# One decode step of attention and a gated feed-forward block: a 224-byte tile below the big slots, and eight tiny loads around the first rows of w_down

## The chip, the core and the metric

The kernel runs on one core of a Trainium2 chip. The metric is the device time of one execution in microseconds (us). Of the kernel before, three runs gave 1369.99, 1370.03 and 1370.04 us, so the median is 1370.03 us. One further execution was taken with the hardware profiler; every duration, wait and load below comes from that one, unless another kernel is named.

## The reference

One token `x` (1 x 576, float32) goes through a layer norm, and the result feeds two blocks whose outputs are added to `x`:

```python
xn = _layernorm(x)
q = (xn @ wq) in 32 heads of 128
p = softmax(q . k_cache * 128**-0.5)        # k_cache: 32 x 16384 x 128
o = (p . v_cache) @ wo                      # v_cache: 32 x 16384 x 128, wo: 4096 x 576
h = gelu(xn @ w_gate) * (xn @ w_up)         # 576 x 4608 each
return x + o + h @ w_down                   # w_down: 4608 x 576
```

Everything is float32. The two caches are 268 MB each, so nearly all of the 588 MB that the kernel reads is read once, used for one or two operations per element, and dropped.

## The kernel before, in words

**Memory.** Small tiles live in one pool (`cpool`) that is allocated first. Behind it lie three big slots of 64 KB in each of the 128 partitions: two from `kpool` (`kslot()`, line 62) and one from `vpool` (`vslot()`, line 65). With the small tiles of this version, the slots begin at byte 27,680 of each partition. 27,680 is 108 x 256 + 32; as every big load starts in its slot at a multiple of 256 bytes and has rows of a multiple of 256 bytes, all of them start 32 bytes past a multiple of 256.

**Loads.** Every big load is one DMA issued by SyncE (SP) through `load` (line 68), and all of these stand in one queue. A load of one head of K or V is 8192 KB: 128 rows, one for each partition, of 65,536 bytes. Sixteen DMA engines take eight rows each, and each engine ends its share by writing the load's semaphore, a packet of 4 bytes. 81 big loads are issued in all.

**Semaphores.** The compiler takes eight DMA semaphores in turn for the loads. A load whose semaphore was last used by a load that nobody is known to have waited for is held back on SP until that earlier load has landed. A load into a slot also waits until the slot's last reader is done.

**Heads.** The loop at line 249 goes over the 32 heads. VectorE multiplies the K slot by the query (`qk`, line 215) and sums it up over 128 elements (line 216), some 17.2 us each; the softmax follows (lines 218 to 230); TensorE then multiplies the V slot by the probabilities (`pv`, line 236), some 10 us. K of head h+1 and V of head h are under way meanwhile. The last head's V goes into a K slot, since no further K follows.

**The end.** Lines 291 to 297 load `w_down` and `wo` into the three slots as they come free. In order: 28 of the 36 row blocks of `w_down` into the V slot (`ta`, 8064 KB), its last 8 into a K slot (`tb`, 2304 KB), 16 row blocks of `wo` behind them (4608 KB), and 8, 4, 2, 1 and 1 row blocks of `wo` into the other K slot (`te`), which holds the last V until `pv` is done with it. Lines 299 to 310 normalise the attention's outputs and turn them into a column (`pot`, then `oT`), lines 312 to 325 multiply `w_down` and `wo` row block by row block on TensorE (`add_out`, line 281), and line 328 copies the sum out for the last DMA, which ScalarE issues.

Of the kernel before, what the change touches and what calls it, by code (L numbers as in the profile page):

```python
# [8 lines left out]
F32 = mybir.dt.float32  # L9
# [4 lines left out]
P = 128  # L14
# [20 lines left out]
QUART = D // 4  # L35
HG = 4
PW = 4 * HG
QH = 4


@with_exitstack
def kernel(ctx: ExitStack, tc: tile.TileContext, x, k_cache, v_cache, wq, wo, wg, wu, wd, out):
    nc = tc.nc
    cpool = ctx.enter_context(tc.tile_pool(name="cpool", bufs=1))
# [15 lines left out]
    wdv = wd.rearrange("(p t) f -> p (t f)", t=WD_T)  # L60

    def kslot():
        return kpool.tile([P, R * DH], F32, tag="k", name="kslot")

    def vslot():
        return vpool.tile([P, R * DH], F32, tag="v", name="vslot")

    def load(dst, src):
        nc.sync.dma_start(dst, src)  # L69
        return dst  # L70
# [5 lines left out]
    row3, tails, at = {}, {}, 0  # L76
# [73 lines left out]
    def q_spread(h):  # L150
        r = 32 * (h // (H // 4))
        lo = h % (H // 4) * DH
        pq = ps_s.tile([P, 512], F32, tag="sm", name="pq")
        nc.tensor.matmul(pq, ones[r : r + 1, :], qrow[r : r + 1, lo : lo + QH * DH], start=True, stop=True)  # L154
        return pq

    def q_take(h, pq):
        qs = spool.tile([P, QH, DH], F32, name="qs", bufs=1)
        nc.scalar.activation(qs.rearrange("p h d -> p (h d)"), pq, AF.Copy)
        for i in range(QH):  # L160
            Q[h + i] = qs[:, i : i + 1, :]
# [41 lines left out]
    S, KT, VT = {}, {}, {}  # L203
    pe = cpool.tile([P, PW - 4 + 32 * PW], F32, name="pe")
    nc.vector.memset(pe, 0.0)
    pe4 = pe[:, PW - 4 :].rearrange("p (k s) -> p k s", s=PW)[:, :, :4]
    lsum = cpool.tile([P, H], F32, name="lsum")
    oall = cpool.tile([P, H], F32, name="oall")

    def qk(h, i, n):  # L210
# [21 lines left out]
    def pv(h):  # L232
        vt, i = VT.pop(h), h % HG
        for k in range(32):
            q, lo = 32 * (k % 4), k * PW + PW - 4 - 4 * i
            nc.tensor.matmul(PO[h // HG % 2][q : q + PW, :], pe[:, lo : lo + PW], vt[:, k * 512 : (k + 1) * 512],  # L236
                             start=i == 0 and k < 4, stop=i == HG - 1 and k >= 28)

    def out_heads(h):
        o4 = spool.tile([P, 512], F32, name="o4", bufs=1)  # L240
        nc.scalar.activation(o4, PO[h // HG % 2], AF.Copy)  # L241
        pc = ps_s.tile([P, 512], F32, tag="sm", name="pc")
        pick = same[:, :PW].rearrange("p (i j) -> p j i", j=4)
        for j in range(4):
# [4 lines left out]
    for h in range(H + 1):  # L249
# [4 lines left out]
        if h > 0:  # L254
            VT[h - 1] = load(vslot() if h < H else kslot(), vv[h - 1])
        more = (h + 1) % QH == 0 and h + 1 < H
        pq = q_spread(h + 1) if more else None
# [29 lines left out]
    def load_rows(t, at, src, lo, n):  # L287
        load(t[:, at * D : (at + n) * D], src[:, lo * D : (lo + n) * D])
        return [t[:, (at + j) * D : (at + j + 1) * D] for j in range(n)]

    ta, tb, te = vslot(), kslot(), kslot()
    a, b = WD_PIECES
    wd_rows = load_rows(ta, 0, wdv, 0, a) + load_rows(tb, 0, wdv, a, b)
    wo_rows, lo = [], 0
    for n in WO_PIECES:
        wo_rows += load_rows(tb, b + lo, wov, lo, n) if lo < WO_A else load_rows(te, lo - WO_A, wov, lo, n)
# [61 lines left out]
```

## Time and profile before

| What | us |
|---|---|
| median of three runs | 1370.03 |
| the profiled execution's own time | 1370.16 |
| its span, first to last instruction | 1368.3 |
| VectorE busy within the span | 1135.8 (83%) |
| TensorE matmuls busy | 406.0 (30%) |
| ScalarE busy | 36.5 (3%) |

The span is 1.9 us shorter than the execution's own time. The page of the profile lists busy times, the DMA engines' share, the DMA queues, and the chain of work that ended last: followed back from the last instruction, at each step to what released it. The chain in order of time gives a start, a duration and what it was; the piece "DMA kslot<-in_A_k_cache_dram" is the time for which nothing but that transfer was being waited for. The timeline gives instructions with the idle time before them and what ended it. The DMA view can be narrowed to a stretch of time; its columns are a queue and its kind, the number of packets that began in the stretch, their MB, and the time that they took as a share of sixteen engines' time in that stretch (so one packet can take over 100% of a very short one).

### The profile page before, as it was taken

The numbers are of one execution on the slowest core, as the hardware profiler recorded it, in microseconds if no ns is written. First come the engines' busy times: TensorE is split into PE (matmuls) and PEld (weight loads), VectorE is DVE, ScalarE is ACT, GpSimd is POOL, SyncE is SP. The second block draws the span as 40 slices with busy tenths as digits, with TensorE's granted clock in tenths as the row PEclk, the third lists the DMA queues.
The fourth block names the chain that finished last, engine by engine and source line by source line (L and its number), as shares of the span: only waits on it lengthen the run. The fifth ranks groups of instructions, "written<-read, shape, count | busy, mean of one in ns | idle before, by whom it ended". The sixth has DMA issues, their size and how long they took to land.

```text
span 1368.3 us, 6377 instructions
## 1 busy us (share of the span) xinstructions
PE 406.0 (30%) x2870; PEld 118.1 (9%) x2870; DVE 1135.8 (83%) x169; ACT 36.5 (3%) x126; POOL 1.0 (0%) x7
## 2 busy tenths in 40 slices
PE   4321233322311232323212332322213333221156
PEld 1110000100000000100000000100001000000012
DVE  1069999899888888898888888998888888988840
ACT  0000000000000000000000000000000000000000
POOL 0000000000000000000000000000000000000000
PEclk8775565565556556565566566565556555665577
DMA  9999999999999999999999999999999999999997
GB/s 404 440 425 450 430 429 430 430 435 432 437 435 429 431 430 439 432 432 435 431 436 433 433 431 430 435 432 439 435 430 430 431 432 437 438 435 428 429 428 336
DMA packets 11704, 588.00 MB, mean 430 GB/s; under 512 B 1303, under 2 KB 1309, under 8 KB 1694
## 3 DMA queue, kind: packets, MB, share of 16 engines
q1 hardware_dynamic: 11664, 587.60, 99.4%
q8 instruction: 22, 0.36, 0.1%
q14 instruction: 4, 0.03, 0.0%
q10 hardware_dynamic: 14, 0.01, 0.0%
HBM read 587.60 MB, written 0.00 MB: 429 GB/s over the span
## 4 chain that ended last, share of the span: by engine, by line
DMA 51%; DVE 46%; PE 2%; issue 0%; SPq 0%; ACT 0%; DVEq 0%
DMA kslot<-in_A_k_cache_dram 41%; DVE s L216 23%; DVE kslot L215 23%; DMA kslot<-in_A_v_cache_dram 3%; DMA kslot<-in_B_w_up_dram 3%; DMA kslot<-in_A_wo_dram 3%; DMA kslot<-in_A_wq_dram 2%; PE pg L139 1%; PE po L236 1%; DVE gu L179 0%; SPq L69 0%; PE pt L222 0%; DVE vslot L176 0%; DVE pm L220 0%; DVE nm L224 0%
## 5 line engine op out<-in xcount | busy, mean ns | idle before, releaser
L215 DVE TENSOR_TENSOR kslot<-kslot,qs 128x16384 f32<-128x16384 f32 (+1 forms) x33 | 551.3, 16705 | 88.4 <-DMA kslot<-in_A_k_cache_dram 86.9
L216 DVE TENSOR_REDUCE s<-kslot 128x128 f32<-128x16384 f32 (+1 forms) x33 | 551.2, 16703 | 3.3
L236 PE MATMUL po<-vslot,pe 128*16 128x512 f32 x1984 | 286.1, 741 | 645.0 <-DMA vslot<-in_A_v_cache_dram 645.0
L236 PEld LDWEIGHTS po<-vslot,pe 128*16 128x16 f32 x1984 | 67.3, 113 | 848.2 <-issue 848.2
L222 PE MATMUL pt<-ident,pm 128*1 128x128 f32 x32 | 11.9, 372 | 236.0 <-DVE pm L220 236.0
L176 DVE TENSOR_TENSOR vslot<-pg,same 128x396 f32<-128x396 f32 (+1 forms) x6 | 3.0, 552 | 69.1 <-PE pg L139 69.1
L139 PE MATMUL pg<-kslot,xnb 128*32 128x396 f32 (+2 forms) x208 | 23.6, 615 | 33.6 <-DMA kslot<-in_B_w_gate_dram 18.9
L228 ACT ACTIVATE nb<-pb 128x1 f32<-128x1 f32 x32 | 5.5, 171 | 812.4 <-PE pb L226 812.4
L320 DVE TENSOR_TENSOR x<-x,po 64x288 f32<-64x288 f32 x1 | 0.5, 457 | 30.8 <-PE po L281 30.8
L222 PEld LDWEIGHTS pt<-ident,pm 128*1 128x1 f32 x32 | 2.5, 79 | 259.4 <-DVE pm L220 218.5
L226 PE MATMUL pb<-nm,ones 1*128 1x1 f32 x64 | 18.1, 350 | 13.2 <-DVE nm L224 13.2
L224 DVE TENSOR_REDUCE nm<-pt 1x1 f32<-1x128 f32 x32 | 8.9, 278 | 14.9 <-PE pt L222 14.9
L226 PEld LDWEIGHTS pb<-nm,ones 1*128 1x128 f32 x64 | 15.8, 305 | 22.2 <-DVE nm L224 11.3
L154 PE MATMUL pq<-qrow,ones 1*128 1x512 f32 x16 | 15.6, 1073 | 0.0
L229 ACT ACTIVATE pe<-s,nb 128x128 f32<-128x128 f32 x32 | 12.8, 401 | 1.0
L302 DVE RECIPROCAL rl<-pl 128x32 f32<-128x32 f32 x1 | 0.4, 358 | 14.9 <-PE pl L300 14.9
L281 PE MATMUL acc<-kslot,oT 128*1 128x144 f32 (+1 forms) x112 | 10.5, 376 | 6.7 <-DMA kslot<-in_A_wo_dram 6.7
L139 PEld LDWEIGHTS pg<-kslot,xnb 128*32 128x32 f32 x208 | 7.1, 126 | 51.0 <-DMA kslot<-in_B_w_gate_dram 19.7
L241 ACT ACTIVATE o<-po 128x512 f32<-128x512 f32 x8 | 4.8, 597 | 222.0 <-PE po L236 222.0
L236 PE MATMUL po<-kslot,pe 128*16 128x512 f32 x64 | 9.6, 769 | 2.6 <-DMA kslot<-in_A_v_cache_dram 2.6
L281 PE MATMUL acc<-vslot,hT 128*1 128x288 f32 x56 | 8.6, 473 | 5.6 <-DMA vslot<-in_B_w_down_dram 5.6
L245 PE MATMUL pc<-same,o 128*128 128x4 f32 x64 | 8.4, 255 | 5.7 <-ACT o L241 5.7
(74 smaller groups left out, 109.9 us busy)
## 6 DMA issues: line engine op xcount, KB each, us to landing
kslot<-in_A_k_cache_dram SPq DMA_DIRECT2D x2, 4096.0 KB
vslot<-in_B_w_down_dram SPq DMA_DIRECT2D x1, 8064.0 KB
kslot<-in_B_w_gate_dram SPq DMA_DIRECT2D x1, 6912.0 KB, 54.0
kslot<-in_B_w_up_dram SPq DMA_DIRECT2D x1, 6912.0 KB
kslot<-in_A_wo_dram SPq DMA_DIRECT2D x1, 4608.0 KB, 39.2
vslot<-in_B_w_gate_dram SPq DMA_DIRECT2D x1, 2304.0 KB, 28.9
vslot<-in_B_w_up_dram SPq DMA_DIRECT2D x1, 2304.0 KB, 37.6
kslot<-in_B_w_down_dram SPq DMA_DIRECT2D x1, 2304.0 KB, 28.7
```

The source lines that it names most:

```text
L139: nc.tensor.matmul(pg[32 * q : 32 * q + 32, b, :size], lhs, rhs[:, lo : lo + size], start=k == 0, stop=k == len(steps) - 1)
L154: nc.tensor.matmul(pq, ones[r : r + 1, :], qrow[r : r + 1, lo : lo + QH * DH], start=True, stop=True)
L215: tc.keep_in_program_order(nc.vector.tensor_mul(blk, blk, Q[h].to_broadcast([P, n, DH])))
L216: nc.vector.tensor_reduce(S[h][:, i : i + n], blk, axis=AX.X, op=ALU.add)
L222: nc.tensor.transpose(pt[:1, :P], pm, ident)
L224: tc.keep_in_program_order(nc.vector.tensor_reduce(nm, pt[:1, :P], axis=AX.X, op=ALU.max, negate=True))
L226: nc.tensor.matmul(pb[:, :1], ones[:1, :], nm, start=True, stop=True)
L228: nc.scalar.activation(nb, pb[:, :1], AF.Copy, scale=SCALE)
L229: nc.scalar.activation(pe4, S.pop(h).rearrange("p (k s) -> p k s", s=4), AF.Exp, bias=nb, scale=SCALE, accum_out=lsum[:, h : h + 1])
L236: nc.tensor.matmul(PO[h // HG % 2][q : q + PW, :], pe[:, lo : lo + PW], vt[:, k * 512 : (k + 1) * 512], start=i == 0 and k < 4, stop=i == ...
L245: nc.tensor.matmul(pc[:, :HG], o4[:, j * DH : (j + 1) * DH], pick[:, j, :], start=j == 0, stop=j == 3)
L281: nc.tensor.matmul(g, lhs, w[:, i * n : (i + 1) * n], start=id(g) not in seen, stop=last)
```

## The change

A tile `pad` of 128 x 56 floats (224 bytes in each partition) is taken from the small tiles' pool. The slots so move up by 224 bytes to byte 27,904, which is 109 x 256.

Eight loads into `pad` are added to the SP queue, which nothing reads. The load with number n takes the first n rows of `w_down` and writes them to partitions 0, 4, 8 and so on; n floats of each row (8 to 32 bytes), and 17 floats (68 bytes) for n = 1. Numbers 1 to 4 stand between the last V and the 28 row blocks of `w_down`, numbers 5 to 8 between these and the last 8. A scheduler orders the instructions of the other engines; the eight loads are held where the program has them. In the built program one matmul changes its place beside that: TensorE's first multiplication of a `w_down` row now stands ahead of the `pot` matmul of line 308 instead of behind it.

```diff
+PAD = 56
...
     lsum = cpool.tile([P, H], F32, name="lsum")
+    pad = cpool.tile([P, PAD], F32, name="pad")
     oall = cpool.tile([P, H], F32, name="oall")
...
     ta, tb, te = vslot(), kslot(), kslot()
     a, b = WD_PIECES
-    wd_rows = load_rows(ta, 0, wdv, 0, a) + load_rows(tb, 0, wdv, a, b)
+    marks = []
+    for n in range(1, 9):
+        at, w = (sum(range(2, n)), n) if n > 1 else (PAD - 17, 17)
+        marks.append((pad[0 : 4 * n : 4, at : at + w], wd[:n, :w]))
+    for m in marks[:4]:
+        tc.keep_in_program_order(nc.sync.dma_start(*m))
+    wd_rows = load_rows(ta, 0, wdv, 0, a)
+    for m in marks[4:]:
+        tc.keep_in_program_order(nc.sync.dma_start(*m))
+    wd_rows += load_rows(tb, 0, wdv, a, b)
```

## The prediction, made before the changed kernel ran

> **What bounds the kernel now.** I read the page's DMA lines first, because 588 MB must come in.
>
> ```profile
> span 1368.3 us, 6377 instructions
> ...
> DMA  9999999999999999999999999999999999999997
> ...
> DMA packets 11704, 588.00 MB, mean 430 GB/s; under 512 B 1303, under 2 KB 1309, under 8 KB 1694
> ...
> q1 hardware_dynamic: 11664, 587.60, 99.4%
> q8 instruction: 22, 0.36, 0.1%
> ...
> DMA 51%; DVE 46%; PE 2%; issue 0%; SPq 0%; ACT 0%; DVEq 0%
> ```
>
> The sixteen DMA engines are at nine tenths or more in every slice but the last, and SP's queue (q1) fills 99.4% of their time. The chain gives VectorE 46%, so the second view was the chain in order of time, to see whether VectorE bounds anything.
>
> ```profile
> 463.17 0.02 issue
> 463.19 17.24 DVE kslot L215
> ...
> 480.52 17.23 DVE s L216
> 497.77 42.84 DMA kslot<-in_A_k_cache_dram
> ...
> 575.28 44.32 DMA kslot<-in_A_k_cache_dram
> ...
> 1197.89 42.77 DMA kslot<-in_A_k_cache_dram
> ...
> 1275.26 42.84 DMA kslot<-in_A_v_cache_dram
> 1318.10 0.14 issue
> ...
> 1329.71 35.08 DMA kslot<-in_A_wo_dram
> 1364.78 0.04 issue
> 1364.83 0.47 PE acc L281 x8
> ...
> 1365.32 0.31 DVE kslot L328
> ```
>
> VectorE's two 17.2 us and one K transfer of 42.8 us make a round of 77.4 us, from 463.19 to about 540.6. In it four loads of 8192 KB land (two K, two V): 33.55 MB in 77.4 us is 433 GB/s, the steady rate of the windows view:
>
> ```profile
> 200.00:700.00 500.00, 140.54 (x901) 38.87 (x901) 451.89 (x53) 13.35 (x49) 0.00 (x0) 0.61 1.00 432
> 700.00:1300.00 600.00, 161.94 (x1051) 45.33 (x1055) 542.77 (x62) 14.85 (x56) 0.00 (x0) 0.61 1.00 433
> ```
>
> The last two columns are the DMA share, 1.00, and GB/s. VectorE is on the chain only because the transfer that a free slot releases waits 42.8 us behind others, though 8192 KB take 77.4/4 = 19.36 us. **So the time is the DMA engines' own work**, begun at about 1.2 us and ended at 1364.78; only 3.5 us follow. An edit counts if it changes what an engine spends on a packet, or lets the queue run dry.
>
> **Part 1: the slots 224 bytes higher.** This touches no instruction, only the address at which each row lands: 27,680 is 32 past a multiple of 256, 27,904 is a multiple. It can act on every data packet: 11,664 less 81 x 16 semaphore packets are 10,368, or 648 for each engine. The price of a packet can be read in very short stretches of the DMA view. From 10.11 to 10.14 us (30 ns, so 480 ns of engine time) one row of the first loads begins, and one semaphore; from 1366.88 to 1366.925 (720 ns of engine time) two 576-byte pieces of the output begin:
>
> ```profile
> q1 hardware_dynamic: 1, 0.07, 503.8%
> q10 hardware_dynamic: 1, 0.00, 1.9%
> ```
> ```profile
> q10 hardware_dynamic: 2, 0.00, 8.6%
> ```
>
> So 65,536 bytes took 5.038 x 480 = 2418 ns, 4 bytes 0.019 x 480 = 9 ns, and 576 bytes 0.086 x 720/2 = 31 ns. Eight rows and a semaphore are 19.353 us, against the 19.36 per load above: there is no gap between loads to win. At the long row's pace (27.1 bytes per ns) 576 bytes need 21 ns, so a data packet has some 10 ns beside its bytes. If the 32 bytes caused all of that, the change would win 648 x 10 ns = 6.5 us. But a semaphore's 4 bytes, far too short to be split by a wrong start, already take 9 ns. That leaves about 1 ns for the start: 648 x 1 ns = 0.65 us. The ends are 0 and -6.5 us (a loss has no reason: the rows stay the same, and the start becomes rounder); I take **-0.6**, nearest to the semaphore's row.
>
> The Trainium skill ("DMA: Bandwidth & Descriptors", section "How a descriptor splits into AXI transactions") says that a transfer not starting on a 256-byte boundary begins at the boundary below and pays for the unused beats of 32 bytes. A 65,536-byte row 32 bytes off would cost one beat more on 2048, an estimate of 0.05%, or 0.7 us over the kernel; by it the sum below would be 0.1 us lower. No run here shows a start on the boundary in a slot.
>
> Compute engines read the slots too, but VectorE's and TensorE's times are covered by the transfers (17.2 + 17.2 us of work per 38.7 us).
>
> **Part 2: eight loads more, on the DMA engines.** A load of n rows is n data packets and n semaphore writes, as the four-row output shows:
>
> ```profile
> DMA packets 8, 0.00 MB, mean 1 GB/s; under 512 B 4, under 2 KB 8, under 8 KB 8
> ```
>
> (four of 576 bytes, four under 512). The eight loads add 36 of each. If an engine takes part in all eight, it gets 8 x (31 + 9) = 0.32 us more; an engine with none gets nothing. Only the engine that ends last counts. They don't end together. From 1353.7 to 1364.9, in 40 slices of 0.28 us:
>
> ```profile
> DMA  9998999978999789999889655554545433332100
> ```
>
> The first engines run dry at about 1360 us, some 5 us ahead of the last. So the cost is 0 if the loaded engine is an early one, +0.32 if it is the last one. The far end comes from the one thing in this trace that disturbs an engine, an instruction fetch (q8, 22 of 16 KB): after one that hits the last engine the K transfer is 44.32 instead of 42.8 us, 1.5 us late. Eight such hits are +12 us. I take **+0.3**, by the rows that are nearest in size.
>
> **Part 3: the same eight loads on SP's queue.** What stands behind them on SP is `w_down` and `wo`.
>
> ```profile
> 1275.26 0.33 SPq L69 DMA_DIRECT2D kslot<-in_A_v_cache_dram  x1
> ...
> 1279.40 17.22 DVE L215 TENSOR_TENSOR kslot<-kslot,qs 128x16384 f32<-128x16384 f32 x1 [3.10 <-DMA kslot<-in_A_k_cache_dram]
> ...
> 1308.00 0.33 SPq L69 DMA_DIRECT2D vslot<-in_B_w_down_dram  x1
> 1313.98 0.33 SPq L69 DMA_DIRECT2D kslot<-in_B_w_down_dram  x1
> ...
> 1314.35 15.79 SPq L69 DMA_DIRECT2D kslot<-in_A_wo_dram  x6
> ...
> 1331.03 0.60 PE L308 MATMUL pot<-same,kslot 128*128 128x32 f32 x2 [1.16 <-DVE kslot L306]
> ...
> 1337.21 0.65 PE L281 MATMUL acc<-vslot,hT 128*1 128x288 f32 x2 [5.57 <-DMA vslot<-in_B_w_down_dram]
> ```
> ```profile
> 1353.73 0.65 PE L281 MATMUL acc<-kslot,oT 128*1 128x288 f32 x2 [6.00 <-DMA kslot<-in_A_wo_dram]
> ...
> 1365.66 0.61 ACTq L329 DMA_DIRECT2D out_dram<-kslot  x1
> ```
>
> Numbers 1 to 4 issue after 1275.6; even at the 0.61 us of the output's issue each they are done long before 1308.00, when the V slot comes free: no cost. Number 5's semaphore was last used by the last K, landed by 1279.40. Number 7 takes that of the last V and so **waits until 1318.10** (the chain's row); number 8 takes that of number 1, which lies right behind that V. The second `w_down` load therefore issues at about 1319 instead of 1313.98. Its cover is the first `w_down` load, under way until 1337.2; even an engine 5 us ahead needs the next rows only at 1332. Slack 13 us, cost nothing. The 8-row `wo` load waits for `pv` as before (about 1328). The 4-row load takes the semaphore of the first `w_down` load, so it and those behind it issue at about 1337.5 to 1339 instead of 1329; queued ahead of them are then 2304 + 4608 + 2304 KB, 21.8 us at 433 GB/s. Cost nothing; without that cover each microsecond of delay would be one of time.
>
> On TensorE the first `w_down` row is now ahead of `pot`, so `oT` is ready at about 1339 instead of 1332. `wo`'s rows want it at 1353.73, after an idle time of 6.00 us; cost nothing.
>
> **The sum.** 1370.16 (1368.3 of span and 1.9 around it) - 0.6 + 0.3 = 1369.9 for a profiled execution; the median shown is 0.13 lower, so **1369.7 us**.
>
> **The rivals.** *A, no change (the forecast).* Both prices are small, whichever engine is last: 0 to -0.65 and 0 to +0.32, so 1369.4 to 1370.4 beside the median of 1370.03.
>
> *B, slower: a tiny packet halts its engine.* The place is the front of `w_down`, on the engine that takes part in all eight loads; the price is a stall per tiny load that the following rows can't hide, up to the fetch's 1.5 us. For it: that fetch costs 1.5 us though its bytes are worth 0.6 us at 27.1 bytes per ns, so a disturbance can cost more than its bytes; and no row here shows a data packet of 8 to 32 bytes. Against: the semaphores are as short, stand in the same queue, and pass in 9 ns. It decides from 2.7/8 = 0.34 us per load, if the engine is the last one. At 0.5 us it gives 1374, at 1.5 us 1382; on the earliest engine its 5 us lead comes off.
>
> The Trainium skill (same page, "Specifications") speaks for B: it gives 512 bytes as the smallest transfer at full rate, below which the DMA engine does a read-modify-write. The trace's 4-byte and 576-byte packets (9 and 31 ns) show no stall of that kind, but none is a short write into a slot's memory that I can name.
>
> *C, faster: the start costs the whole fixed part of a packet.* For it: all 10,368 rows start wrong, and the steady rate is the same for all. Against: the semaphores' 9 ns. At 10 ns a packet 1363.5; at half that 1366.8.
>
> *D, the queue runs dry* because number 7's wait ends later than I read. It would decide only beyond 1332; if the second `w_down` load issued after the first had landed, the gap would be about 2 us (two issues, and the 1.2 us from the output's issue at 1365.66 to its packets at 1366.88): 1372. Speaks against: 1318.10 is a landing in the same order as before.
>
> *E, nothing of it works as said* (the slots don't move, or the tiny loads go elsewhere): 1370.0, inside A.
>
> **How the numbers follow.** A, E and D's milder forms: 0.80; B strong enough for +0.2%: 0.13; C strong enough for -0.2%: 0.07. (0.2%, or 2.7 us, is about what a measurement of this kernel can tell from no change.) So faster 0.07, same 0.80, slower 0.13. The range reaches down into half of C, 1367.0, and up to B at 0.4 us per load, 1373.2, which leaves out about 0.13.
>
> **What would show it.** Part 1: the round of 77.4 us; right if shorter by 0.04 us (32 packets of 1 ns), C if by 0.3 us. Part 2: 72 packets more in q1, 11,736; B if the load behind the eight lands over 19.4 us after the last V. Part 3: SP's rows at about 1319 and 1337 to 1339, and idle times of TensorE at `w_down` and `wo` as before. It would be wrong if the steady rate changes by over 0.2%, or if the DMA share falls below nine tenths between 1318 and 1354.

## The result, and the profile after

The changed kernel takes 1366.55 us (median of ten runs, 1366.42 to 1366.70) against 1370.04 us (ten runs, 1369.86 to 1370.28) of the kernel before: 3.5 us less, a ratio of 0.9974 with a 95% interval of 0.9966 to 0.9983. The forecast was 1369.7 us with a range of 1367.0 to 1373.2, and 0.07 for faster by over 0.2%. The time lies below the range. The profiled execution took 1366.70 us; all that follows on the changed kernel comes from it.

The lines of the changed kernel's page that answer to those shown of the kernel before:

```profile
span 1364.9 us, 6385 instructions
...
DMA  9999999999999999999999999999999999999998
...
DMA packets 11776, 588.00 MB, mean 431 GB/s; under 512 B 1375, under 2 KB 1381, under 8 KB 1766
...
q1 hardware_dynamic: 11736, 587.60, 99.5%
q8 instruction: 22, 0.36, 0.1%
...
DMA 77%; PE 22%; issue 0%; DVE 0%; SPq 0%
```

The span is 3.4 us shorter, q1 has exactly the 72 packets more that were counted, and everything else looks alike. The chain now names TensorE with 22% where it named VectorE with 46%. That is no new bottleneck: in both kernels the chain alternates between transfers and whichever reader released a slot last, and the transfers behind it are always queued. The DMA engines are as full as before. So they do the same work in less time, and the question is on which packets.

**It is gained evenly, long before the tiny loads.** Two rows of the timeline of the kernel before, VectorE's multiplication of two K slots nine heads apart, each released by its K transfer:

```profile
735.78 17.22 DVE L215 TENSOR_TENSOR kslot<-kslot,qs 128x16384 f32<-128x16384 f32 x1 [3.04 <-DMA kslot<-in_A_k_cache_dram]
...
1084.24 17.23 DVE L215 TENSOR_TENSOR kslot<-kslot,qs 128x16384 f32<-128x16384 f32 x1 [3.09 <-DMA kslot<-in_A_k_cache_dram]
```

The same two of the changed kernel:

```profile
733.97 17.23 DVE L217 TENSOR_TENSOR kslot<-kslot,qs 128x16384 f32<-128x16384 f32 x1 [2.93 <-DMA kslot<-in_A_k_cache_dram]
...
1081.62 17.23 DVE L217 TENSOR_TENSOR kslot<-kslot,qs 128x16384 f32<-128x16384 f32 x1 [2.98 <-DMA kslot<-in_A_k_cache_dram]
```

The first starts 1.81 us earlier than before, the second 2.62 us earlier. Between them lie eighteen loads of 8192 KB: 348.46 us before, 347.65 after, so 19.36 and 19.31 us a load, 45 ns less each. (Four of these are the round of 77.4 us: now 77.26.) With eight rows for an engine in a load that is 5 to 6 ns a row.

**A row, averaged over thousands.** The DMA view of the stretch from 700 to 1300 us gives the same from another side. Before:

```profile
DMA packets 4464, 259.60 MB, mean 433 GB/s; under 512 B 496, under 2 KB 496, under 8 KB 496
...
q1 hardware_dynamic: 4455, 259.46, 100.0%
```

After:

```profile
DMA packets 4472, 260.12 MB, mean 434 GB/s; under 512 B 496, under 2 KB 496, under 8 KB 496
...
q1 hardware_dynamic: 4463, 259.98, 100.0%
```

Sixteen engines have 9600 us in this stretch. Of q1's packets 496 are semaphores; 3959 rows before and 3967 after are left, that is 2424.9 and 2420.0 ns of an engine's time for each row with its share of the semaphores and of eight instruction fetches. The difference is 4.9 ns. This count has a weakness: where the stretch begins and ends can shift it by a row for each engine, 16 in 3959 or 0.4%, and the difference is 8 rows.

The packet records of the profile (start, duration and size of each packet) have no such ends. The 8192 rows of 65,536 bytes last 2423.9 ns on average before and 2419.4 after. The records name no engine, but every packet from 100 to 1300 us begins within 16 ns of the end of one other, so the engines can be followed. Those on which no instruction fetch fell need, from one row to the next and with the semaphores' share, 2420.0 ns before (all four) and 2414.9 after (three of five; 2415.2 and 2416.2 the others). Eight of these are the 19.36 and, within 10 ns, the 19.31 us of a load above. That is 5.1 ns a row, and by 648 rows an estimate of 3.3 of the 3.5 us.

**SP's queue did what was worked out.** The end of SP's timeline after the change:

```profile
1271.83 0.33 SPq L70 DMA_DIRECT2D kslot<-in_A_v_cache_dram  x1
1272.21 2.48 SPq L300 DMA_DIRECT2D pad<-in_B_w_down_dram  x4
1304.78 0.37 SPq L70 DMA_DIRECT2D vslot<-in_B_w_down_dram  x1
1305.20 11.16 SPq L303 DMA_DIRECT2D pad<-in_B_w_down_dram  x4
1316.46 0.38 SPq L70 DMA_DIRECT2D kslot<-in_B_w_down_dram  x1
1316.89 18.80 SPq L70 DMA_DIRECT2D kslot<-in_A_wo_dram  x6
```

Tiny loads 1 to 4 issue behind the last V in 2.5 us. Loads 5 to 8 take 11.2 us, because number 7 waits for that V (8.2 us in the list of SP's waits). The second `w_down` load issues 11.7 us after the first instead of 6.0 (1308.00 to 1313.98 before). The row of TensorE's first `w_down` matmul shows that nothing ran dry for it:

```profile
1315.06 9.55 PE L238 MATMUL po<-kslot,pe 128*16 128x512 f32 x64 [2.46 <-DMA kslot<-in_A_v_cache_dram]
...
1333.97 1.12 PE L283 MATMUL acc<-vslot,hT 128*1 128x288 f32 x2 [7.34 <-DMA vslot<-in_B_w_down_dram]
```

From the last V's landing to that of the first `w_down` load are 18.9 us, against 19.0 before (from 1318.24, which is 1318.10 and the 0.14 of issue in the prediction's chain, to its matmul at 1337.21). The 7.34 us of idle time instead of 5.57 come from the `pot` matmul, which now stands behind this row.

The last `wo` loads wait for the first `w_down` load, as was worked out, and issue from 1333.94 on. In the chain of the changed kernel nothing but the `wo` transfers is waited for after these issues:

```profile
1333.94 0.33 SPq L70
...
1335.26 26.08 DMA kslot<-in_A_wo_dram
1361.34 0.04 issue
```

### The profile page after: what moved, and what is told of

It reads as the page before. It is cut to its first block, busy times and chain, and to the rows that moved or that the text cites. A ratio compares the mean times of both kernels' runs of the same rounds, so it can differ in the third digit from the quotient of the medians.

```text
span 1364.9 us, 6385 instructions
## 1 busy us (share of the span) xinstructions
PE 404.6 (30%) x2870; PEld 117.7 (9%) x2870; DVE 1135.8 (83%) x169; ACT 36.5 (3%) x126; POOL 1.0 (0%) x7
## 4 chain that ended last, share of the span: by engine, by line
DMA 77%; PE 22%; issue 0%; DVE 0%; SPq 0%
DMA vslot<-in_A_v_cache_dram 68%; PE po L238 21%; DMA kslot<-in_B_w_up_dram 3%; DMA vslot<-in_B_w_down_dram 2%; DMA kslot<-in_A_wo_dram 2%; DMA kslot<-in_A_wq_dram 2%; PE pg L140 1%; DVE gu L180 0%; SPq L70 0%; DVE vslot L177 0%; PE acc L283 0%; DVE kslot L339 0%
```

## The experiments

Two theories at first. **R**: every row pays for a start off a 256-byte boundary, so the slots' address is the whole gain. **T**: the tiny loads, with the other order that they bring at the end, are the gain. The trace above speaks for R already, as most of the gain lies ahead of the tiny loads; the first two kernels each make one half of the change.

**The address alone.** `lsum` is 56 floats wider, and nothing is issued or moved:

```diff
-    lsum = cpool.tile([P, H], F32, name="lsum")
+    lsum = cpool.tile([P, H + 56], F32, name="lsum")[:, :H]
```

> The slots lie at byte 27,904 as in the changed kernel, but the eight tiny loads are left out and no instruction is added or moved. Theory R (each row pays for its start off a 256-byte boundary, some 5 ns): the whole gain is here, 1366.4 us (0.1 us under the changed kernel, whose tiny loads cost an engine 18 ns each), and the steady round of four loads is 77.28 us against 77.44. Theory T (the tiny loads bring the gain, by another order at the end): 1369.4 to 1370.0 us, round unchanged.

It took 1366.58 us, ratio 0.9975 (0.9965 to 0.9984). The two VectorE rows of its timeline:

```profile
733.75 17.23 DVE L215 TENSOR_TENSOR kslot<-kslot,qs 128x16384 f32<-128x16384 f32 x1 [2.93 <-DMA kslot<-in_A_k_cache_dram]
...
1081.58 17.23 DVE L215 TENSOR_TENSOR kslot<-kslot,qs 128x16384 f32<-128x16384 f32 x1 [2.98 <-DMA kslot<-in_A_k_cache_dram]
```

347.83 us for the eighteen loads, 77.30 us a round. The whole gain is here.

**The tiny loads alone.** The changed kernel with a tile of 256 bytes, so that the slots move to the next place 32 bytes past a boundary:

```diff
-PAD = 56
+PAD = 64
```

> The eight tiny loads as in the changed kernel, but the added tile is 256 bytes instead of 224, so that the slots move by a whole 256 and still start 32 bytes past a boundary. Theory R: 1370.0 to 1370.3 us, round 77.44 us, at most 0.3 us later than the kernel before. Theory T: about 1366.6 us. If the two act together only (a third reading), it is 1370 here and 1370 with the address alone.

1370.07 us, ratio 1.000 (0.9991 to 1.0009). Its rows:

```profile
735.62 17.23 DVE L217 TENSOR_TENSOR kslot<-kslot,qs 128x16384 f32<-128x16384 f32 x1 [3.03 <-DMA kslot<-in_A_k_cache_dram]
...
1084.14 17.23 DVE L217 TENSOR_TENSOR kslot<-kslot,qs 128x16384 f32<-128x16384 f32 x1 [3.11 <-DMA kslot<-in_A_k_cache_dram]
```

348.52 us. T falls: together with the order that they bring, the eight loads gain nothing and cost nothing that can be measured. (A halt on an engine that is ahead of the others could hide in this; the packet records under Part 2 below leave no room for it.)

**Which boundary.** `lsum` wider by 8, 24 and 48 floats puts the slots 64, 128 and 224 bytes past a multiple of 256; the last is the kernel before moved by 192 bytes.

> No tiny loads; the slots start 64 bytes past a multiple of 256 (byte 27,712). If what counts is a 64-byte line in the slots' memory, the gain is all here: 1366.4 us, round 77.28. If it is the 256-byte boundary, whatever the distance: 1370.0, round 77.44. If the cost goes by the bytes that are missing to the boundary: between, or above 1370.

> No tiny loads; the slots start 128 bytes past a multiple of 256 (byte 27,776). A 64-byte or 128-byte boundary as the rule: 1366.4 us, round 77.28. A 256-byte boundary as the rule: 1370.0, round 77.44.

> No tiny loads, whole loads; the slots start 224 bytes past a boundary, so 32 bytes below the next one (byte 27,872). If an engine pays for the unused bytes between the boundary below and the start (7 beats of 32 bytes instead of 1 beat at 32): some 7 ns a row more than at 32, 1374 us. If it pays once for any start off the boundary: 1369.3 to 1370.0, as at 32, 64 and 128.

At 64 bytes it took 1369.43 us, ratio 0.9995 (0.9986 to 1.0004); at 128 bytes 1369.28 us, 0.9994 (0.9985 to 1.0003); at 224 bytes 1370.10 us, 1.000 (0.9991 to 1.0009). The 64-byte and 128-byte boundaries therefore aren't the rule, and a price by the unused bytes below the start isn't either: 224 bytes cost what 32 do, 64 and 128 if anything a little less (0.6 and 0.8 us, inside the intervals of both ratios; the last section comes back to it). The rows at 224 bytes show the old pace, 348.57 us:

```profile
735.58 17.23 DVE L215 TENSOR_TENSOR kslot<-kslot,qs 128x16384 f32<-128x16384 f32 x1 [3.03 <-DMA kslot<-in_A_k_cache_dram]
...
1084.15 17.23 DVE L215 TENSOR_TENSOR kslot<-kslot,qs 128x16384 f32<-128x16384 f32 x1 [3.11 <-DMA kslot<-in_A_k_cache_dram]
```

**Another multiple of 256.** Instead of adding bytes, 32 are saved:

```diff
-    std = cpool.tile([1, 1], F32, name="std")
+    sr = cpool.tile([1, 2], F32, name="sr")
+    std, rstd = sr[:, 0:1], sr[:, 1:2]
...
-    rstd = cpool.tile([1, 1], F32, name="rstd")
```

> No tile added: two one-element tiles share one, which frees 32 bytes, and the slots lie at byte 27,648, a multiple of 256 and of 512. If the 256-byte boundary is the whole rule: 1366.5 us, as at 27,904. If a 512-byte boundary counts too: lower, by up to the same again (1363). If it is the place and not the boundary (27,904 for itself): 1370.

1366.69 us, ratio 0.9975 (0.9966 to 0.9985). It is the boundary and not the place, and a 512-byte boundary adds nothing.

**By the row or by the byte.** The kernel before and the one with the wider `lsum`, both with every K and V load cut into two halves. K's are cut likewise:

```diff
-            VT[h - 1] = load(vslot() if h < H else kslot(), vv[h - 1])
+            VT[h - 1] = vslot() if h < H else kslot()
+            for i in range(0, R, SUB):
+                load(VT[h - 1][:, i * DH : (i + SUB) * DH], vv[h - 1][:, i * DH : (i + SUB) * DH])
```

> The kernel before (slots 32 bytes past a boundary), but every K and V load in two halves of 32,768-byte rows: 144 loads instead of 81, so 1152 rows for each engine instead of 648, with the same bytes. In the two traces so far an aligned load takes 43 ns beside its bytes (8 rows and a semaphore) and one that starts off the boundary 84 ns. If that is paid for each row whatever its length: 63 loads x 84 ns = 5.3 us over the kernel before, 1375.3 us, and 6 us over the same halves on a boundary. If what is lost goes by the bytes: 1372.8, and 3.5 over the aligned halves.

> The same halves with the slots at byte 27,904. By the row: 63 loads x 43 ns = 2.7 us over the aligned kernel with whole loads, 1369.3 us. By the bytes: the same here, so the difference to the halves off the boundary decides (6 against 3.5 us).

Off the boundary it took 1375.44 us, ratio 1.0039 (1.0024 to 1.0055); on it 1369.43 us, ratio 0.9995 (0.9986 to 1.0004). That is 6.0 us between them instead of 3.5, as the price by the row has it; both times are within 0.15 us of what it gave. The DMA view from 700 to 1300 us, off the boundary:

```profile
DMA packets 8881, 258.63 MB, mean 431 GB/s; under 512 B 983, under 2 KB 983, under 8 KB 983
...
q1 hardware_dynamic: 8871, 258.48, 100.2%
```

and on it:

```profile
DMA packets 8924, 259.75 MB, mean 433 GB/s; under 512 B 992, under 2 KB 992, under 8 KB 992
...
q1 hardware_dynamic: 8914, 259.59, 100.2%
```

With the semaphores taken off, 7888 and 7922 rows share the 9600 us: 1217.0 and 1211.8 ns, a difference of 5.2 ns for a row of 32 KB beside 4.9 ns for one of 64 KB, with the same weakness at the ends of the stretch. In the packet records an engine without an instruction fetch needs 1215.3 and 1210.2 ns from row to row, 5.1 ns, the same as for rows of 64 KB. (The recorded 43 and 84 ns are the 19.32 and 19.36 us of a load less its bytes at 27.2 bytes per ns. That is the pace between the rows of 2304 and of 65,536 bytes in the changed kernel's packet records, 93 and 2418 ns.)

This does not hold down to the shortest rows. In the records of the kernel before and the changed one, rows of 18,432 bytes take 688.9 and 686.1 ns and rows of 2304 bytes 95.9 and 93.0 ns (packets over 25 ns above the median left out): some 3 ns each, where the durations of the 64 KB rows differ by 4.6 ns when averaged in the same way.

No version was found that beats the changed kernel: the address alone gives the same time with less code.

## Why the prediction was wrong, point by point

**What bounds the kernel** was right, and so was what follows from it: only what a packet costs, or a queue that runs dry, could count.

**Part 1 failed, in one term.** The step as it stands there: "a semaphore's 4 bytes, far too short to be split by a wrong start, already take 9 ns. That leaves about 1 ns for the start: 648 x 1 ns = 0.65 us." The mechanism was right, the term measured about 5 ns a row and 3.3 us. The sign that the prediction had named for being wrong came too: the steady rate changed by 45 ns in 19.36 us, 0.23%. Two readings went into the term, and both were too rough.

First, the price of a row was read from a single packet, 2418 ns. In the packet records only 31 of the 8192 rows of 65,536 bytes took that, and the average is 2423.9: the one packet was a fast one. The check that was made on it (eight rows and a semaphore are 19.353 us, beside 19.36 a load) seemed to leave no room only because it used that packet. Eight of 2423.9 and a semaphore are 19.40 us, more than the 19.36 that passed: the packets' durations overlap. In the records a packet begins 3 to 4 ns before the one ahead of it on its engine ends, so durations can't be added up to a few ns.

Second, for the same reason the semaphore's 9 ns are not what it costs. In the changed kernel's DMA view a stretch of 53 ns shows four of the tiny loads on one engine, four data packets and four semaphores:

```profile
DMA  0050000040004000040004000040004000040000
...
DMA packets 8, 0.00 MB, mean 2 GB/s; under 512 B 8, under 2 KB 8, under 8 KB 8
...
q1 hardware_dynamic: 8, 0.00, 8.8%
```

Eight packets begin in seven nearly equal steps: the first in slice 3, the last in slice 36, so 33 slices of 1.3 ns for seven steps, 6 ns a step, though each has a duration of some 9 ns (the view's share, 8.8% of 16 x 53 ns, is 75 ns for eight). So a short packet's price on this queue is about 6 ns.

The other side of the subtraction, "some 10 ns beside its bytes", was a 576-byte piece of the output and not a row. Both sides can be read from rows: at 27.2 bytes per ns a row of 65,536 bytes has 13 ns of duration beside its bytes in the kernel before (2422.6 ns, the average of an engine without a fetch) and 8 ns in the changed one (2418.0). So some 5 of 13 ns belonged to the start, not 1 of 10.

The rule of the Trainium skill that the prediction quotes ("DMA: Bandwidth & Descriptors", section "How a descriptor splits into AXI transactions") agrees with the runs on the boundary, 256 bytes; a multiple of 512 brought nothing more. Its account of the price, the beats between the boundary below and the start, does not agree with the runs: one beat at 32 bytes and seven at 224 would be an estimate of 0.7 and 5 us over the kernel, and both cost 3.5 us. (The page speaks of bytes that are fetched; here the address that changed is the one written to.) What an engine does in the 5 ns stays open.

**Part 2 was right in kind, and high.** Forecast +0.32 us on an engine that takes part in all eight loads, by 31 + 9 ns for a load; the lines above show 12 ns a load, 0.1 us in all. Rival B is out: in the packet records of that engine the next row of `w_down` begins 6 ns after the last semaphore behind the tiny packets, and the rows after it, of 64,512 bytes, keep their 2380 ns. (The 9 ns that spoke against B were read in q10, ScalarE's queue, and not in "the same queue" as the text has it; q1's semaphores take 9 ns as well.) The Trainium skill ("DMA: Bandwidth & Descriptors", section "Specifications") names a read-modify-write by the DMA engine below 512 bytes. If it took place here, in packets of 8 to 68 bytes, it cost nothing that shows.

**Part 3 was right**: number 7's wait, its cover by the first `w_down` load, the later `wo` issues, and `pot` behind a `w_down` row, all at no cost.

**The rivals.** What happened is C at half its price, which the text gave as 1366.8 us. It got a chance of 0.07 on the strength of the semaphore's 9 ns alone, and the range's lower end, 1367.0, was drawn from the same. The 0.2 us between 3.3 and 3.5 were not taken apart, nor the shorter rows, which save less than the 5.1 ns that the 3.3 us allow to each.

## What to carry to other kernels

Where the DMA engines bound a kernel, look at where its loads begin in each partition: a small tile more or less ahead of the big ones moves them all, and a start off a multiple of 256 bytes cost some 5 ns for each row of 32 or 64 KB here and some 3 ns for a row of 2 KB, so short rows lose the larger share. Price a packet by the time from one packet to the next on its engine, over thousands of them, never by one packet's duration: durations overlap, and one packet may be a fast one. A plain count in a stretch needs care with the stretch's ends. Small loads for which nobody waited were nearly free in the queue here; what must be checked is the semaphore that they take from a later load.

## What was not expected of the hardware

The rows' durations do not only fall, they become equal: in the packet records nearly all of the 8192 rows of 65,536 bytes spread over 2418 to 2428 ns before, most of them at 2421 and 2428, and after the change 8022 of them take 2418. Starts 32 and 224 bytes past the boundary gave the same spread as each other (4504 and 4494 rows at 2421 ns, 1764 and 1762 at 2428).

Starts 64 and 128 bytes past it gave other spreads and a time 0.6 to 0.8 us lower, which the intervals don't separate from no difference. The records speak for a real one: an engine without an instruction fetch needs 2418.9 and 2418.8 ns from row to row there, 1.1 ns less than at 32 and 224 bytes, which by 648 rows is an estimate of 0.7 us. So the price has a small step within the 256 bytes that none of the readings tried here explains.
